# A retention and mixture-of-experts kernel: state products of attention on four quarters of the array, another order of loads and side work

## The chip, the cores and the metric

The kernel runs on one core of a Trainium2 chip. The metric is the device time of one execution in microseconds (us); lower is better. Times of the profile come from one profiled execution.

## What is computed

Three layers follow one another, all in float32: a linear attention with decay (2 batches, 8 heads, 768 positions, head size 64), a layer of 8 experts that every token passes, weighted by a routing matrix, and a dense layer with `h - tanh(h)`. Cut to what matters:

```
attention, block by block:  out  = ((q k^T) * decay) v + (q * lam^i) state
                            state = lam^64 * state + (k * lam^rev)^T v
experts:   P = exp(x w_gate - max);  8 times: P /= rows sum + 1e-9;  P /= column sum + 1e-9;  P *= N/E
           out = sum over e of P[:, e] * (relu(x w1[e]) w2[e])
dense:     h = x w_in;  out = (h - tanh(h)) w_out
```

The kernel takes blocks of 128 positions in place of 64; the formulas hold for any block.

## The kernel before

**Attention.** `N` = 1536 tokens are cut into 12 chunks `c` of 128 positions; even and odd chunks belong to the two batches. A chunk is one row of `qkv`: q, k with heads on the partitions, k with positions on the partitions, v (256 KB each, 1 MB a chunk). `load_chunk` (L186) puts it into one of four buffers, on SP's queue. The program is written out in order, by hand: what an engine is given stays in that order on it. `prep` (L242) multiplies q by the decay for the state product (`qd`, L246) and scales k (`scale_k`, L252) on GpSimd; for chunks 6 to 9 ScalarE scales k. `scores` (L260) makes q k^T on TensorE into two banks, `decay` (L270) multiplies them by the table `dtab` on VectorE (L273). `states` (L281) makes k^T v (L289). `outputs` (L292) adds the state product (L303: the old state by `qd`, for all but the first chunk of a batch) and the scores by v (L308) in one bank, brings the state up to date on VectorE (L320), copies the output to `xr` on ScalarE (L323) and issues the load of chunk c + 4.

In L303 head 2n sits on partitions 0 to 63 of both operands and of the output, head 2n + 1 on 64 to 127, so two of the four quarters of the array are used:

```
for n in range(NP):
    for hh in range(2):
        p = slice(64 * hh, 64 * hh + 64)
        nc.tensor.matmul(out=o[p, n], lhsT=sn[p, n], rhs=qd[c][p, n], ...)
```

A float32 product is two instructions, so a group of 8 products is 16. Ahead of the loop, five products on zeros (`still`, L397) stand between the scores and the output of chunk 0.

**Side work of attention.** After each chunk the tables `blocks` (L378) and `wt` (L383) give out more. The experts use a scheme with seven products in place of eight, on sums and differences of blocks: `raws` (L336) splits blocks of x into a high and a low half (ScalarE the high, VectorE the low one, L150), `sums` (L344) makes the sums on GpSimd, `sblocks` (L353) splits them. `w_load` (L118) loads a weight unit of 1 MB as two DMAs, `w_sum` (L125) makes its sums, `w1_split` (L152) and `w2_split` (L163) split it. `gate1` (L361) and `gate2` (L370) make the routing logits of four chunks.

**Experts.** A loop over 62 slots (L689) makes seven products of 6 instructions (`product`, L673) and 6 output tiles of 6 (`tiles`, L525). Side work is put into four spots of a slot by `put` (L608): `fd`, `fa`, `fb`, `fc` in this order. `stage` (L455) makes the routing matrix in slots 1 to 5, with a column sum by TensorE (L471) and VectorE. `conv` (L494) turns the weights of the dense layer to float32, with steps on VectorE and GpSimd (L514, L515). In slot 0, `pah` is the sum of `pal` and `sa` (L723), `pal` is then added to by the fourth product, and two relus empty the banks (L587).

Of the kernel before, what the change touches and what calls it, by code (L numbers as in the profile page):

```python
# [21 lines left out]
NCH = N // CH  # L22
# [32 lines left out]
def kernel(  # L55
# [17 lines left out]
    psh = ctx.enter_context(tc.tile_pool(name="psh", bufs=4, space=bass.MemoryType.PSUM))  # L73
    psy = ctx.enter_context(tc.tile_pool(name="psy", bufs=1, space=bass.MemoryType.PSUM))
# [42 lines left out]

    def w_load(q):  # L118
# [3 lines left out]
        for i in range(2):  # L122
            nc.sync.dma_start(out=wraw[q][:, 1024 * i:1024 * i + 1024], in_=src[:, 1024 * i:1024 * i + 1024])
# [54 lines left out]
    attq = ctx.enter_context(ExitStack())  # L178
    ap = attq.enter_context(tc.tile_pool(name="att", bufs=1, side="right"))
# [4 lines left out]
    qkvt = {}  # L184

    def load_chunk(c, parts=((0, 2), (2, 4))):  # L186
        if c not in qkvt:
            qkvt[c] = yq.tile([128, 4, 512], F32, tag="qkv", name=f"qkv{c}")
        src = qkv[c].rearrange("p (a n) -> p a n", a=4)
        for i, j in parts:  # L190
            nc.sync.dma_start(out=qkvt[c][:, i:j], in_=src[:, i:j])
# [12 lines left out]
    warm = bank("warm")  # L204
    for i in range(9):
        nc.tensor.matmul(out=warm, lhsT=zero[:, 0:128], rhs=zero, start=True, stop=True)
# [45 lines left out]
    def scale_k(c):  # L252
        kn = qkvt[c][:, 2].rearrange("p (h d) -> p h d", h=H)
# [5 lines left out]

    def scores(c):  # L260
        k = qkvt[c][:, 1].rearrange("p (n i) -> p n i", n=NP)
        sc = [bank(f"sc{c}_{i}") for i in range(2)]
        q = qkvt[c][:, 0].rearrange("p (n i) -> p n i", n=NP)
        for n in range(NP):
            for hh in range(2):
                p = slice(64 * hh, 64 * hh + 64)
                nc.tensor.matmul(out=sc[hh][:, 128 * n:128 * n + 128], lhsT=k[p, n], rhs=q[p, n], start=True, stop=True)
        scps[c] = sc

    def decay(c):  # L270
        a = ap2.tile([128, H, 128], F32, tag="at", name=f"at{c}")
# [619 lines left out]
```

## Time and profile before

| | |
|---|---|
| time, median of 3 runs | 1256.54 us (1256.02 to 1257.32) |
| profiled execution | 1257.17 us, span of the profile 1255.4 us |
| TensorE, weight load, VectorE, ScalarE, GpSimd busy | 99%, 91%, 77%, 44%, 34% of the span |
| attention | from the start to 55.10 us |
| experts | from 55.10 us on, 62 slots |
| DMA | 83.53 MB, mean 67 GB/s; 327 GB/s in the first 31 us |

Busy time is how long an engine has work in it; the ends of products are modelled, and following products overlap, so the time from one start to the next tells more than a duration. In a row of the timeline an idle time in brackets is that ahead of the group, with what ended it; a name that had been done for long stands for something else, often a DMA.

### The profile page before, as it was taken

The page shows a single profiled execution, that of the slowest core. Times are in us where ns is not written, and L with a number is a line of the kernel's source. Part 1 is how long each engine was busy: PE and PEld are TensorE (multiplying, and loading weights), DVE is VectorE, ACT ScalarE, POOL GpSimd, SP SyncE. Part 2 cuts the span into 40 slices and gives each one's busy share as a digit, 9 for nine tenths or more (in the row PEclk, how much of TensorE's full clock was granted, in tenths as well). Part 3 has the DMA queues.
Part 4 walks back from the last instruction along what each step waited for, and adds up shares of the span by engine and source line. Part 5 has one row for each costly group of instructions (what it writes and reads, how often), then busy time and mean ns, then how long its engine had stood idle before and what let it go on. Part 6 is the DMA issues. An engine that isn't in the chain of part 4 may idle for free.

```text
span 1255.4 us, 18456 instructions
## 1 busy us (share of the span) xinstructions
PE 1245.5 (99%) x7031; PEld 1139.2 (91%) x7031; DVE 969.4 (77%) x1874; ACT 547.2 (44%) x1044; POOL 424.6 (34%) x428
## 2 busy tenths in 40 slices
PE   9999999999999999999999999999999999999998
PEld 6889999999999999999999999999999988888887
DVE  6967888778777677777777777767775688898987
ACT  3753333333333333333333333333333578786864
POOL 5832233334433343343334334334332202020200
PEclk9999999999999999999999999999999999999999
DMA  8310112212112221221222112222211111011101
GB/s 327 129 34 34 43 59 74 69 60 72 59 60 85 81 83 59 68 64 59 72 72 72 59 59 73 68 78 90 68 55 34 34 34 34 34 35 34 34 34 67
DMA packets 35658, 83.53 MB, mean 67 GB/s; under 512 B 4209, under 2 KB 12401, under 8 KB 35569
## 3 DMA queue, kind: packets, MB, share of 16 engines
q1 hardware_dynamic: 35424, 82.35, 20.0%
q8 instruction: 55, 0.90, 0.3%
q14 instruction: 35, 0.28, 0.1%
q10 hardware_dynamic: 144, 0.00, 0.0%
HBM read 70.80 MB, written 11.53 MB: 66 GB/s over the span
## 4 chain that ended last, share of the span: by engine, by line
PE 95%; DVE 3%; ACT 2%; DMA 0%; issue 0%; SPq 0%; DVEq 0%; ACTq 0%
PE yq L534 13%; PE yq L536 13%; PE yq L535 13%; PE pal L679 7%; PE pal L681 6%; PE pal L682 6%; PE pbh L681 3%; PE pbh L682 3%; PE pbh L679 3%; PE yp L565 3%; PE g L813 3%; PE yp L563 3%; PE yp L562 3%; PE g L815 3%; PE g L814 3%; PE pbl L681 2%
## 5 line engine op out<-in xcount | busy, mean ns | idle before, releaser
L549 DVE SCALAR_TENSOR_TENSOR yacc<-yq,prob,yacc 128x512 f32<-128x512 f32 x336 | 240.2, 746 | 115.9 <-PE yq L536 115.3
L150 POOL TENSOR_TENSOR w1l<-wsum,w1h 128x1024 fp32r<-128x1024 f32 x31 | 74.1, 2391 | 214.1 <-ACT w1h L148 214.1
L534 PE MATMUL yq<-w2h,h1h 128*128 128x512 f32 x384 | 146.1, 381 | 0.0
L536 PE MATMUL yq<-w2h,h1l 128*128 128x512 f32 x384 | 145.6, 379 | 0.0
L535 PE MATMUL yq<-w2l,h0h 128*128 128x512 f32 x384 | 145.6, 379 | 0.0
L536 PE MATMUL yq<-w2h,h0l 128*128 128x512 f32 x384 | 145.6, 379 | 0.0
L535 PE MATMUL yq<-w2l,h1h 128*128 128x512 f32 x384 | 145.6, 379 | 0.0
L534 PE MATMUL yq<-w2h,h0h 128*128 128x512 f32 x384 | 145.6, 379 | 0.0
L150 POOL TENSOR_TENSOR w2l<-wraw,w2h 128x512 fp32r<-128x512 f32 x80 | 105.9, 1339 | 80.5 <-ACT w2h L148 80.5
L679 PE MATMUL pal<-xsh,w1h 128*128 128x384 f32 x384 | 125.6, 327 | 1.6 <-ACT sa L707 0.9
L682 PE MATMUL pal<-xsh,w1l 128*128 128x384 f32 x384 | 125.2, 326 | 0.0
L681 PE MATMUL pal<-xsl,w1h 128*128 128x384 f32 x384 | 125.2, 326 | 0.0
L587 ACT ACTIVATE h1h<-pah 128x384 fp32r<-128x384 f32 x64 | 31.4, 491 | 184.6 <-PE yq L535 180.0
L514 POOL TENSOR_TENSOR c<-c,d 128x256 f32<-128x256 f32 x64 | 47.4, 741 | 185.0 <-DVE d L513 185.0
L587 ACT ACTIVATE h0h<-pbl 128x384 fp32r<-128x384 f32 x64 | 31.4, 491 | 139.1 <-PE yq L535 139.0
L536 PEld LDWEIGHTS yq<-w2h,h0l 128*128 128x128 f32 x384 | 72.7, 189 | 10.3
L534 PEld LDWEIGHTS yq<-w2h,h0h 128*128 128x128 f32 x384 | 72.7, 189 | 10.3
L535 PEld LDWEIGHTS yq<-w2l,h0h 128*128 128x128 f32 x384 | 72.6, 189 | 10.2
L536 PEld LDWEIGHTS yq<-w2h,h1l 128*128 128x128 f32 x384 | 72.6, 189 | 10.2
L535 PEld LDWEIGHTS yq<-w2l,h1h 128*128 128x128 f32 x384 | 72.7, 189 | 6.9
L534 PEld LDWEIGHTS yq<-w2h,h1h 128*128 128x128 f32 x384 | 72.6, 189 | 6.9
L679 PEld LDWEIGHTS pal<-xsh,w1h 128*128 128x128 f32 x384 | 72.6, 189 | 5.4 <-DVE pah L723 1.0
(220 smaller groups left out, 3253.7 us busy)
## 6 DMA issues: line engine op xcount, KB each, us to landing
wraw<-in_w SPq DMA_DIRECT2D x64, 512.0 KB, 4.9
d<-in_wio SPq DMA_DIRECT2D x64, 256.0 KB, 5.2
qkv<-in_qkv SPq DMA_DIRECT2D x21, 512.0 KB, 7.1
wscr<-c SPq DMA_DIRECT2D x64, 128.0 KB, 1.9
wraw<-wscr SPq DMA_DIRECT2D x16, 512.0 KB, 4.4
out<-yacc SPq DMA_DIRECT2D x12, 256.0 KB, 2.2
qkv<-in_qkv SPq DMA_DIRECT2D x4, 256.0 KB, 5.4
lamb<-in_lam ACTq DMA_DIRECT2D x1, 4.0 KB, 4.9
```

The lines of the kernel that those rows point to most:

```text
L150: eng.tensor_tensor(out=lo, in0=src, in1=hi.bitcast(F32), op=ALU.subtract)
L514: nc.gpsimd.tensor_tensor(out=c1.bitcast(F32), in0=c1.bitcast(F32), in1=lo.bitcast(F32), op=ALU.mult)
L534: nc.tensor.matmul(out=yp, lhsT=hi, rhs=pairs(w2h[q][:, i]), start=i == 1, stop=False)
L535: nc.tensor.matmul(out=yp, lhsT=hi, rhs=pairs(w2l[q][:, i]), start=False, stop=False)
L536: nc.tensor.matmul(out=yp, lhsT=lo, rhs=pairs(w2h[q][:, i]), start=False, stop=i == 0)
L549: nc.vector.scalar_tensor_tensor(out=y, in0=yp, scalar=prob[:, c, q // 4:q // 4 + 1], in1=y, op0=ALU.mult, op1=ALU.add)
L562: nc.tensor.matmul(out=yp, lhsT=a[:, ts], rhs=pairs(w2h[q][:, i]), start=first, stop=False)
L563: nc.tensor.matmul(out=yp, lhsT=a[:, ts], rhs=pairs(w2l[q][:, i]), start=False, stop=False)
L587: nc.scalar.activation(out=hi, in_=ps, func=ACTF.Relu)
L679: nc.tensor.matmul(out=ps, lhsT=w1h[q][:, ws], rhs=pairs(xh[:, k]), start=start and k == 0, stop=False, skip_group_check=True)
L681: nc.tensor.matmul(out=ps, lhsT=w1h[q][:, ws], rhs=pairs(xl[:, k]), start=False, stop=False, skip_group_check=True)
L682: nc.tensor.matmul(out=ps, lhsT=w1l[q][:, ws], rhs=pairs(xh[:, k]), start=False, stop=k == 1, skip_group_check=True)
```

## The change

State products take four quarters of the array: heads are put on the partitions in another order, so that the four products of a set have four pairs of row half and column half. The two row halves write to two banks (`ps[:, 0]`, `ps[:, 1]`), whose upper halves hold the states' new parts and the gate's products. The order in `outputs` becomes scores by v, k^T v, state product, gate. x comes out with its heads in another order, so the rows of `w1` and of the gate's weights are put in that order as they are loaded (`by_head`: four DMAs with pieces of 512 bytes for `w1`, 32 bytes for the gate). q and k of a chunk have a buffer apart from k and v, and q and k are issued a chunk earlier. Weights 0 are issued behind chunk 3, ahead of chunk 4, and their split comes one to three chunks earlier; `w_load(1)` moves from chunk 6 to 4, `w_sum(1)` from 9 to 7. The `still` products go. `decay` is one pass over both banks. `sums(10)` and `raws(7)` move into slot 0 of the experts, the last gate's products from spot `fc` to `fa` of slot 0, `raws(8)` and `sums(11)` from `fc` of slot 0 to `fd` of slot 1. The column sum of the routing matrix is taken by VectorE over the 12 chunks first, and TensorE then sums 8 columns in place of 96. The banks of attention are given back at its end, and the experts' banks wait for them tile by tile.

```diff
+    def by_head(dst, src, n):
+        d, s = (a.rearrange("p (b k f) -> p b k f", b=n, k=2) for a in (dst, src))
+        for e in range(2):
+            for r in range(2):
+                nc.sync.dma_start(out=d[64 * e:64 * e + 64, :, r], in_=s[64 * r:64 * r + 64, :, e])
+
...
-        for i in range(2):
+        if u < NU:
+            by_head(wraw[q][:, 0:1024], src[:, 0:1024], 4)
+        for i in range(u < NU, 2):
             nc.sync.dma_start(out=wraw[q][:, 1024 * i:1024 * i + 1024], in_=src[:, 1024 * i:1024 * i + 1024])
...
-    load_chunk(0, ((0, 1), (1, 2), (2, 4)))
-    for c in range(1, 4):
-        load_chunk(c)
-    nc.sync.dma_start(out=wgt, in_=wg.rearrange("p (k e) -> p k e", e=E))
+    load_chunk(0, (0, 1), (1, 2))
+    load_chunk(1, (0, 2))
+    load_chunk(0, (2, 4))
+    load_chunk(2, (0, 2))
+    load_chunk(1, (2, 4))
+    load_chunk(3, (0, 2))
+    for c in (2, 3):
+        load_chunk(c, (2, 4))
+    by_head(wgt.rearrange("p k e -> p (k e)"), wg, 2)
+    w_load(0)
...
+        q, k = (qkt[c][:, i].rearrange("p (n i) -> p n i", n=NP) for i in range(2))
+        scps[c] = psc.tile([128, 2, 512], F32, tag="sc", name=f"sc{c}")
         for n in range(NP):
-            for hh in range(2):
-                p = slice(64 * hh, 64 * hh + 64)
-                nc.tensor.matmul(out=sc[hh][:, 128 * n:128 * n + 128], lhsT=k[p, n], rhs=q[p, n], start=True, stop=True)
-        scps[c] = sc
+            for r in range(2):
+                p = slice(64 * r, 64 * r + 64)
+                nc.tensor.matmul(out=scps[c][:, r, 128 * n:128 * n + 128], lhsT=k[p, n], rhs=q[p, n], start=True, stop=True)
...
+        at[c] = ap2.tile([128, H, 128], F32, tag="at", name=f"at{c}")
+        nc.vector.tensor_tensor(out=byrow(at[c]), in0=scps.pop(c).rearrange("p r (n i) -> p r n i", n=NP), in1=byrow(dtab),
+                                op=ALU.mult)
...
+        ps = ops[c] = pso.tile([128, 2, 512], F32, tag="o", name=f"o{c}")
+        o = ps[:, :, 0:256].rearrange("p r (a i) -> p r a i", a=2)
+        for i in range(H):
+            a, r, e = i // 4, i // 2 % 2, i % 2
+            h = 4 * a + 2 * e + r
+            nc.tensor.matmul(out=o[64 * e:64 * e + 64, r, a], lhsT=v[:, h], rhs=at[c][:, h], start=a == 0, stop=first,
+                             skip_group_check=True)
+        if carried(c):
+            stp = ps[:, 0, 256:512].rearrange("p (n e) -> p n e", n=NP)
+            for n in range(NP):
+                for r in range(2):
+                    h = 2 * n + r
+                    nc.tensor.matmul(out=stp[64 * r:64 * r + 64, n], lhsT=k[:, h], rhs=v[:, h], start=False, stop=True,
+                                     skip_group_check=True)
...
         if not first:
...
+            for a in range(2):
+                for r in range(2):
+                    for e in range(2):
+                        p, n = slice(64 * r, 64 * r + 64), 2 * a + e
+                        nc.tensor.matmul(out=o[64 * e:64 * e + 64, r, a], lhsT=sn[p, n], rhs=qd[c][p, n], start=False, stop=True,
+                                         skip_group_check=True)
+        gates(c)
...
-                nc.vector.tensor_copy(out=sn, in_=stp.pop(c))
+                nc.vector.tensor_copy(out=sn, in_=stp)
...
+        nc.scalar.activation(out=xr[c].rearrange("p (a r) i -> p r a i", r=2), in_=o, func=ACTF.Copy)
+        for i in (4, 5) if c == 0 else (c + 5,):
+            if i < NCH:
+                load_chunk(i, (0, 2))
         if c + 4 < NCH:
-            load_chunk(c + 4, ((0, 2), (2, 4)) if carried(c + 4) else ((0, 2), (3, 4)))
+            load_chunk(c + 4, (2, 4) if carried(c + 4) else (3, 4))
...
+    def gates(c):
+        b, ps = c // TPB - 1, ops[c][:, 1, 256:512]
+        if b >= 0 and c % TPB == 0:
+            gate1(b, ps)
+        if b >= 0 and c % TPB == 1:
+            gate2(b, ps)
+
+    def gatesc(c):
+        b, ps = c // TPB - 1, ops.pop(c)[:, 1, 256:512]
+        if b >= 0 and c % TPB == 0:
+            gate1c(ps)
+        if b >= 0 and c % TPB == 1:
+            gate2c(b, ps)
...
-        10: [(raws, 6), (sums, 9)], 11: [(raws, 7), (sums, 10)],
+        10: [(raws, 6)], 11: [(sums, 9)],
...
-        1: lambda: w_load(0),
-        3: lambda: (w_sum(0, nc.vector), w1_split(0, 0, which=(0,)), w2_split(0, 0)),
-        4: lambda: w1_split(0, 0, which=(1,)), 5: lambda: w2_split(0, 1), 6: lambda: (w1_split(0, 1), w_load(1)),
-        9: lambda: w_sum(1, nc.gpsimd),
+        2: lambda: (w_sum(0, nc.vector), w1_split(0, 0), w2_split(0, 0)),
+        3: lambda: (w1_split(0, 1), w2_split(0, 1)), 4: lambda: w_load(1), 7: lambda: w_sum(1, nc.gpsimd),
...
     ahead(0)
-    still = psy.tile([128, 512], F32, tag="y3", name="still")
-    for i in range(5):
-        nc.tensor.matmul(out=still, lhsT=zero[:, 0:128], rhs=zero, start=True, stop=True)
+    ahead(1)
     make_lq()
     for c in range(NCH):
         for i in ((1,), (2, 3))[c] if c < 2 else (c + 2,):
             if i < NCH:
...
-        if c == 1:
-            ahead(1)
-            ahead(2)
-        if c > 0:
-            states(c)
         outputs(c)
+        gatesc(c)
...
-        if 0 < c < NCH - 2:
-            scores(c + 2)
-        if c > 0 and c % TPB == 0:
-            gate1(c // TPB - 1)
-        if c > TPB and c % TPB == 1:
-            gate2(c // TPB - 1)
-        if 0 < c < NCH - 2:
-            decay(c + 2)
+        ahead(c + 2)
...
+    psh = ctx.enter_context(tc.tile_pool(name="psh", bufs=4, space=bass.MemoryType.PSUM, reuse_waits="tile"))
+    psy = ctx.enter_context(tc.tile_pool(name="psy", bufs=1, space=bass.MemoryType.PSUM, reuse_waits="tile"))
...
+        box["part"] = sm.tile([128, E], F32, tag="cp", name="cp")
+        nc.vector.tensor_reduce(out=box["part"], in_=prob.rearrange("p t e -> p e t"), axis=AX.X, op=ALU.add)
...
-            nc.tensor.matmul(out=ps[:, 0:NCH * E], lhsT=ones, rhs=prob.rearrange("p t e -> p (t e)"),
-                             start=True, stop=True)
+            nc.tensor.matmul(out=ps[:, 0:E], lhsT=ones, rhs=box.pop("part"), start=True, stop=True)
             cs = sm.tile([128, E], F32, tag="cs", name="cs")
-            nc.vector.tensor_reduce(
-                out=cs, in_=ps[:, 0:NCH * E].rearrange("p (t e) -> p e t", e=E), axis=AX.X, op=ALU.add
-            )
-            nc.vector.tensor_scalar(out=cs, in0=cs, scalar1=1e-9, scalar2=None, op0=ALU.add)
+            nc.vector.tensor_scalar(out=cs, in0=ps[:, 0:E], scalar1=1e-9, scalar2=None, op0=ALU.add)
...
-    put(fc, 0, gate1, NBLK - 1, ybank)
-    put(fc, 0, raws, NCH - 4)
-    put(fc, 0, sums, NCH - 1)
+    gps = {}
+
+    def lastgate(i):
+        if i % 2 == 0:
+            gps[i] = ybank(f"lg{i}")
+        if i == 0:
...
+    put(fa, 0, lastgate, 0)
+    put(fa, 0, raws, NCH - 5)
+    put(fb, 0, lastgate, 1)
+    put(fb, 0, sums, NCH - 2)
     put(fc, 0, sblocks, NCH - 3)
-    put(fd, 1, gate2, NBLK - 1, ybank)
+    for i in (2, 3):
+        put(fd, 1, lastgate, i)
+    put(fd, 1, raws, NCH - 4)
+    put(fd, 1, sums, NCH - 1)
     put(fa, 1, stage, 0)
```

## Rows read from the trace of the kernel before

**Rows 1.** Busy time by stage: us, PE, PEld, DVE, ACT, POOL, granted clock, DMA share, GB/s.

```profile
10.46:55.10 44.64, 43.54 (x756) 37.34 (x756) 39.40 (x79) 26.57 (x71) 35.42 (x33) 1.00 0.72 259
```

**Rows 2.** TensorE in order of time: start us, us, engine, line, operation, count, idle before.

```profile
6.34 2.08 PE L267 MATMUL sc<-qkv 64*128 64x128 f32 x16 [0.87 <-DMA qkv<-in_qkv]
...
8.36 2.10 PE L399 MATMUL still<-zr 128*128 128x512 bf16 x5
...
10.39 1.09 PE L308 MATMUL o<-at,qkv 128*64 128x128 f32 x16
...
19.29 1.16 PE L267 MATMUL sc<-qkv 64*128 64x128 f32 x16
...
20.38 0.69 PE L289 MATMUL stp<-qkv 128*64 128x64 f32 x16
...
20.99 1.09 PE L303 MATMUL o<-qd,st 64*64 64x128 f32 x16
...
22.01 1.09 PE L308 MATMUL o<-at,qkv 128*64 128x128 f32 x16
...
28.41 1.06 PE L365 MATMUL lgT<-xr,wgt 128*8 128x128 f32 x32
...
55.10 0.43 PE L679 MATMUL pal<-xph,w1h 128*128 128x384 f32 x1
```

**Rows 3.** DMA in 40 slices of 0 to 30 us; SP's issues: start us, us.

```profile
GB/s 0 0 115 141 34 165 267 426 421 415 415 421 426 421 415 404 415 371 320 320 289 344 333 246 197 279 393 366 339 377 415 426 388 415 410 382 415 415 284 339
...
12.04 0.80 SPq L191 DMA_DIRECT2D qkv<-in_qkv  x2
```

**Rows 4.** GpSimd in order of time, 19 to 55 us.

```profile
19.31 1.28 POOL L246 TENSOR_TENSOR qd<-qkv,lq 128x512 f32<-128x512 f32 x1 [2.51 <-PE o L308]
...
46.45 1.17 POOL L348 TENSOR_TENSOR xr<-xr,xr 128x256 f32<-128x256 f32 x1
...
50.09 1.50 POOL L246 TENSOR_TENSOR qd<-qkv,lq 128x512 f32<-128x512 f32 x1
...
51.55 0.73 POOL L129 TENSOR_TENSOR wsum<-wraw 128x256 f32<-128x256 f32 x1
...
54.20 1.06 POOL L132 TENSOR_TENSOR wsum<-wraw,wsum 128x256 f32<-128x256 f32 x1
```

**Rows 5.** GpSimd by line and shape, 5 to 80 us: busy us, mean ns, idle before.

```profile
L246 POOL TENSOR_TENSOR qd<-qkv,lq 128x512 f32<-128x512 f32 x10 | 14.7, 1476 | 4.1 <-PE o L308 2.5 <-DVE lq L229 1.0 <-PE o L303 0.6
...
L258 POOL TENSOR_TENSOR qkv<-qkv,dtab 128x512 f32<-128x512 f32 x6 | 6.5, 1079 | 7.1 <-DVE dtab L217 6.5 <-DMA qkv<-in_qkv 0.6
...
L150 POOL TENSOR_TENSOR w2l<-wraw,w2h 128x512 fp32r<-128x512 f32 x3 | 4.2, 1389 | 12.0 <-ACT w2h L148 12.0
```

**Rows 6.** VectorE in order of time, 35 to 53 us.

```profile
35.54 1.28 DVE L273 TENSOR_TENSOR at<-sc,dtab 128x512 f32<-128x512 f32 x2
...
42.37 1.75 DVE L150 TENSOR_TENSOR w1l<-wsum,w1h 128x1024 fp32r<-128x1024 f32 x1
...
51.15 1.28 DVE L273 TENSOR_TENSOR at<-sc,dtab 128x512 f32<-128x512 f32 x2
```

**Rows 7.** Waits of TensorE, 0 to 120 us: us, times, longest.

```profile
PE pal L679 <- ACT sa L707: 0.9, 1, 0.9
...
PE pal L679 <- DVE pah L723: 0.7, 1, 0.7
```

**Rows 8.** ScalarE by line and shape, 5 to 80 us.

```profile
L368 ACT ACTIVATE lt<-lgT 8x128 f32<-8x128 f32 x12 | 3.2, 266 | 2.5 <-PE lgT L365 2.4
```

**Rows 9.** Chain that ended last, in order of time: start us, us.

```profile
95.72 0.31 PE mxB L465 x2
...
104.98 0.19 PE csum L471 x2
```

**Rows 10.** GpSimd in order of time in the experts, 322 to 329 us.

```profile
322.01 0.73 POOL L129 TENSOR_TENSOR wsum<-wraw 128x256 f32<-128x256 f32 x1 [4.43 <-DMA wraw<-in_w]
...
328.10 0.74 POOL L514 TENSOR_TENSOR c<-c,d 128x256 f32<-128x256 f32 x1 [3.18 <-DVE d L513]
```

More of the change, by code (lines that the diff above doesn't have):

```diff
@@ L203 @@
     nc.vector.memset(ones, 1.0)
-    warm = bank("warm")
+    warm = pso.tile([128, 2, 512], F32, tag="o", name="warm")
     for i in range(9):
-        nc.tensor.matmul(out=warm, lhsT=zero[:, 0:128], rhs=zero, start=True, stop=True)
+        nc.tensor.matmul(out=warm[:, 0], lhsT=zero[:, 0:128], rhs=zero, start=True, stop=True)
     nc.vector.memset(bias[:, 3:4], 0.0)
@@ L294, in outputs @@
         first, last = pos == 0, pos == NPB - 1
-        v = qkvt[c][:, 3]
-        sn = st[c % B]
-        o = psy.tile([128, 512], F32, tag=f"y{2 + c % 2}", name=f"o{c}").rearrange("p (n i) -> p n i", n=NP)
-        if not first:
-            for n in range(NP):
-                for hh in range(2):
-                    p = slice(64 * hh, 64 * hh + 64)
-                    nc.tensor.matmul(out=o[p, n], lhsT=sn[p, n], rhs=qd[c][p, n], start=n == 0, stop=False,
-                                     skip_group_check=True)
@@ L305, in outputs @@
-        for n in range(NP):
-            for hh in range(2):
-                h = 2 * n + hh
-                nc.tensor.matmul(
-                    out=o[64 * hh:64 * hh + 64, n], lhsT=v[:, 64 * h:64 * h + 64], rhs=at[c][:, h],
-                    start=first and n == 0, stop=True, skip_group_check=True,
-                )
-        if c == 0:
-            states(0)
+        kv, sn = kvt[c], st[c % B]
+        k, v = (kv[:, i].rearrange("p (h d) -> p h d", h=H) for i in range(2))
+        ps = ops[c] = pso.tile([128, 2, 512], F32, tag="o", name=f"o{c}")
@@ L317, in outputs @@
             else:
[L318 removed]
                 for n in range(NP):
[L320 removed]
+                    nc.vector.scalar_tensor_tensor(out=sn[:, n], in0=sn[:, n], scalar=lq[:, n, 127:128], in1=stp[:, n],
                                                    op0=ALU.mult, op1=ALU.add)
         xr[c] = ap8.tile([128, KT, 128], F32, tag="xr", name=f"xr{c}")
[L323 removed]
+        nc.scalar.activation(out=xr[c].rearrange("p (a r) i -> p r a i", r=2), in_=o, func=ACTF.Copy)
@@ L359, with gate1 @@
     nc.gpsimd.memset(lt, 0.0)
-    def gate1(b, bank=bank):
-        ps = bank(f"lgT{b}")
+    def gate1(b, ps):
         for k in range(KT):
@@ L365, in gate1, with gate1c, gate2, gate2c @@
                 nc.tensor.matmul(out=ps[32 * j:32 * j + E, 0:128], lhsT=wgt[:, k], rhs=xr[TPB * b + j][:, k],
-                                 start=k == 0, stop=k == KT - 1)
+                                 start=k == 0 and b == NBLK - 1, stop=k == KT - 1, skip_group_check=True)
+    def gate1c(ps):
         for j in range(TPB):
             nc.scalar.activation(out=lt[32 * j:32 * j + E], in_=ps[32 * j:32 * j + E, 0:128], func=ACTF.Copy)
-    def gate2(b, bank=bank):
-        ps = bank(f"lg{b}")
-        nc.tensor.matmul(out=ps[:, 0:TPB * E], lhsT=lt, start=True, stop=True,
+    def gate2(b, ps):
+        nc.tensor.matmul(out=ps[:, 0:TPB * E], lhsT=lt, start=b == NBLK - 1, stop=True, skip_group_check=True,
                          rhs=ident.rearrange("p (j r) -> p j r", j=TPB)[:, :, 0:E])
+    def gate2c(b, ps):
         nc.scalar.activation(out=logits[:, TPB * b:TPB * b + TPB], in_=ps[:, 0:TPB * E].rearrange("p (j e) -> p j e", e=E),
                              func=ACTF.Copy)
+    def gates(c):
[10 more added lines that the diff above has]
+            gate2c(b, ps)
     blocks = {
```

55 lines of the change are left out of this document (21 added, 34 removed).

## The prediction

> **What bounds the kernel now.** I read the busy time by stage first. From 10.46 to 55.10 us TensorE is busy for 43.54 of 44.64 us, but VectorE has 39.40 and GpSimd 35.42 [rows 1]. Attention thus has three engines near their limit, and the experts behind it are a stream of TensorE work. I then read TensorE in order of time: twelve chunks follow one another, and the first expert product begins at 55.10 [rows 2]. That instant, call it T, is what the change can move; the 1200 us behind it follow at TensorE's pace. Third, I read GpSimd and VectorE over the same stretch, since time taken from TensorE alone is no time taken from T [rows 4 to 6].
>
> **State products on four quarters (L303).** Today's 16 instructions alternate between two quarters and take from 20.99 to the next group's 22.01, 1.02 us [rows 2]. Ten chunks have them. No row has four quarters. Nearest are the gate's products on four column groups, 32 in 1.06 us, so 0.53 for 16, and L289, 16 with weights as wide in 0.61 us (20.38 to 20.99) [rows 2]. The other end is 1.02, if they do not overlap. I take 0.6, as L289 loads the same width of weights: 10 x 0.42 = 4.2 us less TensorE work, of which only nine chunks lie behind the load discussed below.
>
> **The start.** The five `still` products go (8.36 to 10.39 [rows 2]) and the scores of chunk 1 take their place, so that those of chunks 1 and 2 no longer follow output 0 together. TensorE reaches the scores of chunk 4 at about 18 instead of 19.29: 2.0 us come from `still`, less the waits for VectorE, which now has decay(1) ahead of its scans. The price may be the clock. The scores of chunk 0 take 2.08 us against 1.09 for later ones (19.29 to 20.38), and a `still` product 0.41 us for 512 columns, which is 1.2 GHz; the group at 10.39 is the first at 2.4 GHz [rows 2]. The granted clock reads 1.00 in the stages [rows 1], so here the spacing is what tells. I expect the rise at the same place, since TensorE is as continuously occupied from 6.34 on; a late rise costs at most half of what runs before 18.
>
> **The load order.** Weights 0 (1 MB) now go ahead of chunk 4. Before, chunk 4 was issued at 12.04 [rows 3] and its q was first used at 19.31, after 2.51 us in which GpSimd sat idle [rows 4], which ends with the load and not with the engine named. The 16 slices of 0.75 us up to 12 us add up to 3365 KB, and those up to 19.3 to 5640 KB [rows 3]. Chunk 4's q and k end at 4720 KB, so a load is usable some 920 KB after its bytes. Now they end at 5770 KB: (5770 + 920 - 3365) / 418 KB per us = 8.0 us behind 12, at 20.0 if the queues stay full. The slices between 13.5 and 19.5 sank to 197 because little was queued until 12.04; that gap closes. Half of weights 0 and the gate's weights come in pieces of 512 and 32 bytes, and no row has such loads. From below they cost nothing; from above 1 MB at the slowest slice, 197, which is 2.8 us more. I take 1.0, since a full queue ran at 415 to 426: usable at 21.0. TensorE then idles about 3 us where it had no wait, and is 1.7 us late at the scores of chunk 4.
>
> The Trainium skill ("DMA: Bandwidth & Descriptors", Specifications) puts line rate at pieces of 512 bytes and up. By that rule only the gate's weights would pay, and chunk 4 would be usable near 20.0.
>
> **GpSimd, the next bound.** It has `w_sum(1)` moved ahead of its last two scalings of q (qd), which TensorE needs. The k and v of chunk 4 come 1.05 MB behind its q (2.5 us), at 23.5; scaling k ends at 24.6 (1.08 [rows 5]). What follows on its queue up to qd 11 is 7 x qd, 3 x `sums`, 2 x `w2l`, one scaling of k and one `w_sum`. At the means of [rows 5], with 3.64 for `sums` (46.45 to 50.09) and 3.71 for `w_sum` (51.55 to 55.26) [rows 4], that is 7 x 1.48 + 10.9 + 2.8 + 1.1 + 3.7 = 28.9. At the shortest seen, 1.28 for qd and 4 x 0.73 for the other two [rows 4], it is 9.0 + 8.7 + 2.8 + 1.1 + 2.9 = 24.5. I take 27.3, nearer the upper end, because VectorE works beside it as now. qd 11 is ready at 51.9, 0.3 later than today's 51.59 [rows 4], and only the last state products (0.6) follow: T = 52.5 instead of 55.10.
>
> **The other two at that point.** TensorE: the scores of chunk 4 from 21.0 (1.1), then for chunks 3 to 9 each 1.02 + 0.61 + 0.6 and a later chunk's scores, 1.09 (7 x 3.32 = 23.2), the gate twice (1.06 each, and some 0.6 for its transposed product in all), and 1.6 for each of the last two: 21.0 + 1.1 + 23.2 + 2.7 + 3.2 = 51.2, and about 1 of waits for VectorE. VectorE: decay(7) ended at 36.82 and decay(11) at 52.43, with the low half of weights 0 (1.75) between them [rows 6]. That is now done earlier, as the weights are there earlier. It takes its time there, so decay(7) stays near 36.8; decay(11) ends near 52.43 - 1.7 - 0.3 (one pass over two banks instead of two) = 50.4, and output 11 with its states adds 1.6: 52.0. The three agree within half a microsecond. T is 52.5 by GpSimd: **2.6 us gained**.
>
> **Slots 0 and 1 of the experts.** TensorE waits 0.7 us for `pah` and 0.9 for `sa` [rows 7]. The last gate's products (1.06) move into the first wait, so about 1.0 goes. `sa` was late behind four copies for the gate (266 ns each [rows 8]) and the blocks of chunks 8 and 9, part of which now come half a slot later: 0.9 goes. In return those copies and raws(7) stand ahead of two relus on ScalarE, 1.1 + 0.7 us, so that the bank of `pal` comes free some 1.0 later than slot 1 wants it. Net 0.9 gained, between 1.9 and a loss of 1.
>
> **Routing sums.** The product for 96 columns takes 0.19 us on the chain; one of a single column takes 0.31, both as two instructions [rows 9]. Fewer columns need not be shorter: 0, at best 8 x 0.1 = 0.8. VectorE's passes stay as many; the reduction only moves ahead of the product.
>
> **Weight loads later on.** The 32 loads become five issues each, one half in 512-byte pieces. GpSimd waits 4.43 us for such a load already, and after its sums has 3.18 us until its next work is released [rows 10]. Three more issues of 0.4 [rows 3], and half a weight at the slowest rate (1.4), make 2.6: covered by the 3.18, so nothing. SP's stores and loads queued behind come 1.2 us later; without that cover this would be rival 4.
>
> **The sum.** 2.6 + 0.9 = 3.5. The profiled execution took 1257.17 us (span 1255.4); the median of the runs is 1256.54. That gives 1253.7 on the profile's own scale and **1253.0** against the median.
>
> **The rivals.**
> 1. *Loads at full rate.* If the pieces run like whole rows, chunk 4 is usable at 20.0, GpSimd is less disturbed (24.5 to 26), and T comes down to 50.5 to 51.5, TensorE's bound with chunk 4 one us earlier. With 1.5 from the slots that is 5 to 6 us: 1250.8. For it: full queues ran at 415 and more [rows 3]. Against: VectorE's own 52.0. The sentence of the skill above speaks for it.
> 2. *The idle costs the clock.* TensorE idles from 18 to 21 or later. Only a rise is in the trace, after 4 us of work behind a gap near 1 [rows 2]. If the clock falls there, chunks 3 and 4 run at 1.2 GHz and some 4 us of work take 4 us more, of which about 2 reach T, since GpSimd waits on loads too; with chunk 4 at 22.8 as well, T is 55.5 and the slots give 0.8 at most: 1256.2. The Trainium skill ("TensorE: Matmul & The Clock Gate", Part 1) says an idle array goes back to the lower clock; no row here shows a fall.
> 3. *The quarters don't overlap.* Then 0.42 comes back for each of nine chunks: TensorE ends at 55.0, and 0.9 of the slots with 0.1 of T is left: 1255.5. Against it: four column groups do overlap, at 33 ns an instruction [rows 2].
> 4. *Slower: the weights come late all the way.* GpSimd's conversion steps stand behind its sums. From 3.2 us of delay of a load on they are late; VectorE is in order and empties TensorE's banks, and I put the point from which TensorE stalls at about 5 us. At 5.5 this is 0.5 for each of some 29 loads, 14 us, less the 3.5: 1267. Against it: it needs twice the delay of the upper bound.
>
> **Chances.** GpSimd as the bound 0.40 (1251.5 to 1255), full rate 0.25, clock or late loads 0.20, quarters 0.05, slower 0.10. Two tenths of a per cent, about what a measurement of this kernel can tell from no change, is 2.5 us: faster means below 1254.0. The first case lies there with 0.27, the second wholly, the third with 0.03: faster 0.55. Late loads that add up past 1259 take 0.03 beside the 0.10: slower 0.13. The rest, 0.32, is the same. The range runs from 1249.5 (T 50, slots 1.9) to 1258 (T 56.5 with a fallen clock, nothing in the slots); it leaves out rival 4 and the ends of the others.
>
> **What would show it.** The first `pal` product near 52.5, just behind the last state products, and these just behind a qd 11 that ends near 52. The L303 group in 0.5 to 0.6 us. A wait of about 3 us for q of chunk 4 from 18 to 21. No wait for `sa` in slot 1. GpSimd waiting 5 to 7 us for weights instead of 4.43, with its next step released as now. I am wrong if chunk 4 is there no later than today, if VectorE rather than GpSimd ends last before T, if the spacing of products falls back to 1.2 GHz, or if TensorE shows any new wait behind slot 3.

## The result, and the profile after

The change makes the kernel slower: 1271.0 us in the median (1270.47 to 1272.81), 1.0116 of the time before (95% interval 1.0098 to 1.0133). The profiled execution took 1271.25 us, span 1269.1. The forecast was 1253.0 us, range 1249.5 to 1258.0.

Nearly all of it is lost ahead of the experts: T, the start of the first `pal` product, comes at 67.73 us instead of 55.10, 12.6 later. Taking each slot by the start of its first copy `sa`, slot 0 stands 12.56 us behind the kernel before and slot 1 10.63; the distance then grows to 10.9 at slot 6, 12.9 at slot 12, 13.3 at slot 40 and 13.56 at the end.

The stage from output 0 to T, to be read against [rows 1] (columns as there):

```profile
10.29:67.73 57.44, 43.80 (x741) 37.86 (x741) 37.61 (x71) 26.12 (x71) 34.40 (x34) 0.87 0.59 206
```

TensorE, VectorE and GpSimd have hardly more to do than before, or less (43.54, 39.40 and 35.42 us then), but take 57.44 us instead of 44.64 for it. No engine is near its limit any more: they wait for each other. Whom TensorE and ScalarE wait for, 5 to 68 us (us in total, times, longest):

```profile
PE sc L281 <- DMA qk<-in_qkv: 7.2, 2, 5.6
PE o L372 <- ACT xr L328: 3.0, 2, 1.9
PE o L303 <- ACT kv L270: 2.8, 1, 2.8
PE o L380 <- ACT lt L377: 2.3, 1, 2.3
...
ACT xr L328 <- DVE st L325: 23.8, 8, 11.0
```

Before, the last line did not exist: ScalarE's copy of the outputs waited for TensorE alone. The same view of the kernel before (5 to 62 us), and the copy of chunk 3 in order of time:

```profile
ACT xr L323 <- PE o L308: 20.5, 8, 8.9
...
25.77 1.09 PE L308 MATMUL o<-at,qkv 128*64 128x128 f32 x16
...
26.91 0.60 ACT L323 ACTIVATE xr<-o 128x512 f32<-128x512 f32 x1 [0.27 <-PE o L308]
```

That copy followed its product (25.77 and 1.09) within 0.1 us. In the changed kernel it waits for VectorE's state update in each of eight chunks. Such a sum counts all the idle time ahead of the copies, so 23.8 us is not what the update costs. The changed kernel in order of time, 12 to 36 us, all engines (start us, us, engine, line; idle time before, with what ended it):

```profile
12.41 4.97 SPq L120 DMA_DIRECT2D wraw<-in_w  x4
...
17.42 0.60 SPq L129 DMA_DIRECT2D wraw<-in_w  x1
...
17.60 0.67 PE L317 MATMUL o<-qd,st 64*64 64x128 f32 x16
...
18.14 0.83 SPq L200 DMA_DIRECT2D qk<-in_qkv  x2
...
23.85 2.08 PE L281 MATMUL sc<-qk 64*128 64x128 f32 x16 [5.58 <-DMA qk<-in_qkv]
...
25.86 1.97 PE L303 MATMUL o<-at,kv 128*64 128x128 f32 x16
...
27.81 1.52 DVE L135 TENSOR_TENSOR wsum<-wraw 128x256 f32<-128x256 f32 x1
...
28.61 0.71 PE L317 MATMUL o<-qd,st 64*64 64x128 f32 x16
...
31.11 1.16 DVE L138 TENSOR_TENSOR wsum<-wraw,wsum 128x256 f32<-128x256 f32 x1
...
31.83 0.67 PE L317 MATMUL o<-qd,st 64*64 64x128 f32 x16
...
32.43 0.40 PE L372 MATMUL o<-xr,wgt 128*8 128x128 f32 x6
...
33.13 0.84 DVE L325 SCALAR_TENSOR_TENSOR st<-st,lq,o 128x64 f32<-128x64 f32 x4
...
34.07 0.60 ACT L328 ACTIVATE xr<-o 128x512 f32<-128x512 f32 x1 [11.03 <-DVE st L325]
...
34.72 1.09 PE L372 MATMUL o<-xr,wgt 128*8 128x128 f32 x26 [1.89 <-ACT xr L328]
```

Three things can be read here. SP issues q and k of chunk 4 only at 18.14, behind weights 0, whose four pieces alone take it 4.97 us (12.41), and TensorE waits 5.58 us for them. VectorE's sums of weights 0 (27.81 to 32.2) stand ahead of the state update at 33.13. And the copy of the output of chunk 3 waits for that update, with the gate's products behind it: the last product of this output ends at 29.32 (28.61 and 0.71), the copy starts at 34.07. So 4.75 of the 11.03 us are the update's; the rest is TensorE's late chunk. The experiments tell what each is worth.

### The profile page after: what moved, and what is told of

The parts are those of the page before. It is cut to its first block, busy times and chain, and to the rows that moved or that the text cites. A ratio compares the mean times of both kernels' runs of the same rounds, so it can differ in the third digit from the quotient of the medians.

```text
span 1269.1 us, 18726 instructions
## 1 busy us (share of the span) xinstructions
PE 1245.2 (98%) x7026; PEld 1139.1 (90%) x7026; DVE 969.3 (76%) x1862; ACT 548.9 (43%) x1044; POOL 424.6 (33%) x428
## 4 chain that ended last, share of the span: by engine, by line
PE 89%; DVE 5%; ACT 2%; DMA 2%; SPq 1%; issue 1%; POOL 1%; DVEq 0%; ACTq 0%; POOLq 0%
PE yq L543 12%; PE yq L545 12%; PE yq L544 12%; PE pal L706 6%; PE pal L709 6%; PE pal L708 6%; PE pbh L706 3%; PE pbh L708 3%; PE yp L574 3%; PE pbh L709 3%; PE g L840 3%; PE yp L571 3%; PE yp L572 3%; PE g L842 3%; PE g L841 3%; PE pbl L709 2%
## 5 line engine op out<-in xcount | busy, mean ns | idle before, releaser
L544 PEld LDWEIGHTS yq<-w2l,h0h 128*128 128x128 f32 x384 | 72.6, 189 | 10.3
L543 PEld LDWEIGHTS yq<-w2h,h0h 128*128 128x128 f32 x384 | 72.6, 189 | 10.3
L545 PEld LDWEIGHTS yq<-w2h,h1l 128*128 128x128 f32 x384 | 72.6, 189 | 10.3
L545 PEld LDWEIGHTS yq<-w2h,h0l 128*128 128x128 f32 x384 | 72.6, 189 | 10.3
L135 POOL TENSOR_TENSOR wsum<-wraw 128x256 f32<-128x256 f32 x31 | 22.7, 731 | 170.5 <-DMA wraw<-in_w 170.5
```

The lines of the kernel that those rows point to most:

```text
L543: nc.tensor.matmul(out=yp, lhsT=hi, rhs=pairs(w2h[q][:, i]), start=i == 1, stop=False)
L544: nc.tensor.matmul(out=yp, lhsT=hi, rhs=pairs(w2l[q][:, i]), start=False, stop=False)
L545: nc.tensor.matmul(out=yp, lhsT=lo, rhs=pairs(w2h[q][:, i]), start=False, stop=i == 0)
```

## Experiments

The suspects: the loads (**A**: weights in pieces, more of SP's time), the shared tile (**B**: one tile `ps` holds outputs, new states and gate, read by ScalarE and VectorE), and, once the first runs were in, the early work on weights 0. T and times of all kernels follow. T is that of the profiled execution; each ratio is taken against executions of the kernel before that were timed with it, whose medians lie between 1256.6 and 1257.2:

| kernel | T, us | median us | ratio to before (95% interval) |
|---|---|---|---|
| before | 55.10 | 1256.6 | |
| the change | 67.73 | 1271.0 | 1.0098 to 1.0133 |
| 1 plain loads | 66.74 | 1268.2 | 1.0068 to 1.0102 |
| 2 states in banks of their own | 60.44 | 1263.3 | 1.0034 to 1.0064 |
| 3 = 1 + 2 | 57.35 | 1258.6 | 1.0001 to 1.0019 |
| 4 first pieces on ScalarE's queue | 68.83 | 1272.7 | 1.0105 to 1.0145 |
| 5 copy ahead of the state update | 62.19 | 1265.4 | 1.0055 to 1.0089 |
| 6 weights 0 as before | 61.80 | 1269.8 | 1.0091 to 1.0124 |
| 7 = 1 + 5 | 59.55 | 1260.5 | 1.0016 to 1.0038 |
| 8 = 1 + 5 + 6 | 56.83 | 1258.2 | 1.0001 to 1.0019 |
| 9 = 8 + gate copies ahead | 53.47 | 1253.8 | 0.9963 to 0.9984 |
| 10 before + pieces | 58.48 | 1263.2 | 1.0029 to 1.0061 |
| 11 = 9 with the late copies | 59.80 | 1260.7 | 1.0023 to 1.0047 |
| 12 = 9 with the early weights | 56.04 | 1258.5 | 1.0004 to 1.0024 |

**1. Plain loads.** The host puts the rows of `w1` and of the gate's weights into the new order, and the loads are whole again.

```diff
-        if u < NU:
-            by_head(wraw[q][:, 0:1024], src[:, 0:1024], 4)
-        for i in range(u < NU, 2):
+        for i in range(2):
...
-    by_head(wgt.rearrange("p k e -> p (k e)"), wg, 2)
+    nc.sync.dma_start(out=wgt, in_=wg.rearrange("p (k e) -> p k e", e=E))
```

> The changed kernel with its rows of w1 and of the gate's weights put in the new order by the host's layout, so that each weight load is two DMAs of whole 4 KB rows again and the gate's load one. Theory A (the five issues of a load by heads hold up SP: chunk 4's q and k are issued at 18.1 instead of about 11, TensorE stands 5.6 us and its clock falls, and later the dense layer's loads behind a weight load come late, 2.9 us over the slots): chunk 4's scores begin at 18 to 20 without a fall of the clock behind them, the first pal product comes 6 to 8 us earlier than 67.7, the steps in the slots (2.0 at slot 12, 0.4 at slot 40, 0.25 at slot 6) go, and the time is 1260 to 1263. Theory B (output and states in one bank put ScalarE's copy behind VectorE's state update, and this chain sets the length of attention): the load is only waited for once, the chain is as long as before from there, the first pal product comes at 64 or later, and the time is 1265 to 1267, since only the slots come back.

Measured 1268.2, 2.8 less than the change and above both ranges. TensorE, in order of time:

```profile
21.12 1.90 PE L279 MATMUL sc<-qk 64*128 64x128 f32 x16 [3.14 <-DMA qk<-in_qkv]
```

Chunk 4 comes 2.7 us earlier than with pieces, yet T moves by 1.0 only: TensorE arrives earlier at a chain that is late for another reason. In the slots, slot 12 loses 0.70 instead of 1.97, but in the profiled execution 1.72 us are lost at slot 34, where the change lost nothing (last section). T of 66.74 is what B had forecast (64 or later), so B is the larger cause.

**2. States in banks of their own.** The states' new parts get a tile; to make room, the scores have one pair of banks instead of two.

```diff
-    psc = attq.enter_context(tc.tile_pool(name="psc", bufs=2, space=bass.MemoryType.PSUM))
+    psc = attq.enter_context(tc.tile_pool(name="psc", bufs=1, space=bass.MemoryType.PSUM))
+    pss = attq.enter_context(tc.tile_pool(name="pss", bufs=2, space=bass.MemoryType.PSUM))
...
-            stp = ps[:, 0, 256:512].rearrange("p (n e) -> p n e", n=NP)
+            stp = pss.tile([128, 512], F32, tag="st", name=f"stp{c}")[:, 0:256].rearrange("p (n e) -> p n e", n=NP)
...
-                    nc.tensor.matmul(out=stp[64 * r:64 * r + 64, n], lhsT=k[:, h], rhs=v[:, h], start=False, stop=True,
+                    nc.tensor.matmul(out=stp[64 * r:64 * r + 64, n], lhsT=k[:, h], rhs=v[:, h], start=n == 0, stop=True,
```

> The changed kernel with the states' new parts in a bank of their own (two such banks; the scores then have one pair of banks instead of two). Loads by heads stay. Theory B: ScalarE's copy of an output no longer waits for VectorE's state update, its scaling of k and its copies for the gate come earlier, and TensorE's waits for the copy, for scaled k and for the gate's copies (3.0, 2.8 and 2.3 us) go: 6 to 9 us less before the first pal product, 1262 to 1265. Theory A: those waits came only from the late load and from the half clock; they shift elsewhere, at most 2 us less, 1269 or more. The single pair for the scores may cost up to 1 us.

Measured 1263.3, 7.7 less, as B had it. TensorE's waits, 5 to 62 us:

```profile
PE sc L282 <- DVE at L289: 5.7, 3, 2.4
PE sc L282 <- DMA qk<-in_qkv: 4.9, 2, 3.2
```

No wait of TensorE for ScalarE is left. The first line comes from the single pair of score banks, so 7.7 may understate the tile; by how much, this run does not show.

**3. Both.**

> Both of these: layout by the host, and states in a bank of their own. If A and B together are all that went wrong, what was forecast for the quarters should be seen: first pal product at 50 to 53, no fall of the clock, 1250 to 1254. If TensorE's clock or GpSimd's queue is a third cause, the first pal product stays at 55 or later and the time is 1255 to 1259.

Measured 1258.6, in the range that stood for a third cause. The wait for chunk 4 is gone, since TensorE itself comes to it later (its scores start at 21.25 without idle time, 21.12 in run 1). TensorE waits 7.2 us for VectorE to empty the only pair of score banks, the longest time 3.74 behind the sums of weights 0.

**4. The first pieces on ScalarE's queue.** The gate's weights and weights 0 are issued there, so that SP is free for chunk 4.

> The changed kernel with the first loads by heads (the gate's weights and the first half of weights 0) issued on ScalarE's queue instead of SP's; the pieces and their bytes are the same. If the time of SP's issues is what made chunk 4 late, its q and k are issued by 9 us and land by 16 to 19, and the first pal product comes 4 to 7 us earlier: 1264 to 1267, as the later loads stay on SP. If the small pieces themselves slow the DMA engines, chunk 4 lands at 22 to 24 as now, and the time stays at 1270 to 1272.

Measured 1272.7: no faster than the change. Chunk 4 was waited for 0.39 us only, but now k and v of chunk 0 (1.97 us, to 10.96) and q and k of chunk 2 (2.38 us, to 15.62) came late, and from 10 to 15 us the DMA engines moved 205 GB/s at full share (1.13) instead of 379 at 1.01 in the kernel before. SP's time is thus not all of it: the pieces take the DMA engines' time, whoever issues them.

**5. The copy ahead of the state update.** In `outputs` the lines of ScalarE's copy move ahead of VectorE's update. Nothing else.

```diff
         gates(c)
+        xr[c] = ap8.tile([128, KT, 128], F32, tag="xr", name=f"xr{c}")
+        nc.scalar.activation(out=xr[c].rearrange("p (a r) i -> p r a i", r=2), in_=o, func=ACTF.Copy)
         if not last:
...
-        xr[c] = ap8.tile([128, KT, 128], F32, tag="xr", name=f"xr{c}")
-        nc.scalar.activation(out=xr[c].rearrange("p (a r) i -> p r a i", r=2), in_=o, func=ACTF.Copy)
```

> The changed kernel with one edit: in every chunk ScalarE's copy of the outputs is issued ahead of VectorE's state update, so that in the bank that both read it is VectorE that waits for ScalarE (copy 0.60 us) and no longer ScalarE for VectorE; loads, banks and weights stay. Theory bank (the copy's wait for the state update, which stands behind VectorE's other work, is most of the lost time): the waits of the copy on VectorE go, the first pal product comes near 61 instead of 67.7, and the time is 1261 to 1265. Rival (any order of the two on one bank costs the same, the wait only passes to VectorE, which is as full): 1268 to 1272.

Measured 1265.4, T 62.19, 0.4 us above the theory's range and clear of the rival's. The order of two lines is worth 5.6 us. The gate's copies, still behind the update, wait for it now: those to `lt` 5.9 us in two places, those to `logits` 1.8 in two.

**6. Weights 0 as before.** `w_load(0)` behind chunk 1, and the table `wt` of the kernel before.

> The changed kernel with weights 0 as in the kernel before: loaded after chunk 1, sums and splits of weights 0 spread over chunks 3 to 6, weights 1 loaded at chunk 6 and summed at chunk 9; banks and by-head loads stay. Theory load order and VectorE's early weights work together: chunk 4's queries and keys are issued some 5 us earlier, the wait of 5.58 us for them falls under 1 us, and no sums stand ahead of decay 5, so the first pal product comes at 59 to 62 and the time is 1262 to 1266. Rival (the shared bank alone sets the end, whatever VectorE does ahead of the state update): 1268 to 1271.

Not as expected: T falls to 61.80 as the theory had it, and chunk 4 is waited for 0.29 us; but the median is only 1.2 us lower, and its runs spread from 1266.9 to 1272.0. The profiled one is the fastest (1266.92, span 1264.8), and even there 4.6 us are lost again behind slot 1, in steps at slot 12 (1.97), slot 18 (1.62) and later.

**7. Plain loads, copy ahead.**

> The changed kernel with the order of e5_order and the plain loads of e1_plain (the host lays the rows out, no by-head pieces); both pairs of score banks stay, weights 0 stay early. If the 7.2 us in which TensorE waited for the single pair of score banks in e3_both were a cost of that experiment alone: first pal product at 54 to 56, time 1254 to 1257. If VectorE's early work on weights 0 (sums of 1.2 to 1.5 us each instead of 0.42 before) is what is left: 57 to 58 as in e3_both, 1257.5 to 1260.

Measured 1260.5, T 59.55, above both ranges: with both pairs of score banks the kernel is not faster than run 3. The gate's copies still stand behind the update here, so the tile costs more than the order of this one copy. What the 7.2 us of waits cost run 3 this run can't tell; run 12, which is this kernel with the gate's copies ahead, comes to 1258.5 and T 56.04, against 1258.6 and 57.35.

**8. All three.**

> The changed kernel with all three taken back or mended: copy ahead of the state update, plain loads, weights 0 loaded and worked on as in the kernel before. What is left of the change is the quarters, the moved scores and slots, and the routing sums. If the three are all that was lost, the prediction's sum of 3.5 us holds for the rest: first pal product at 52 to 54, time 1252.5 to 1255.5. If the rest has a cost of its own (the clock at half after a gap, single tiles), 1256 to 1260.

Measured 1258.2. T is 56.83, not 52 to 54, so something was left. All engines of this kernel, 31 to 37 us:

```profile
31.24 0.60 ACT L318 ACTIVATE xr<-o 128x512 f32<-128x512 f32 x1
...
33.95 0.84 DVE L324 SCALAR_TENSOR_TENSOR st<-st,lq,o 128x64 f32<-128x64 f32 x4
...
34.83 0.20 ACT L381 ACTIVATE logits<-o 128x32 f32<-128x32 f32 x1 [2.99 <-DVE st L324]
34.92 2.00 ACT L267 ACTIVATE kv<-kv,dtab 128x64 f32<-128x64 f32 x8
36.03 1.09 PE L300 MATMUL o<-at,kv 128*64 128x128 f32 x16 [2.46 <-ACT kv L267]
```

The gate's copy of 0.20 us waits 2.99 us for the state update, ScalarE's scaling of k stands behind it, and TensorE waits for k. The gate's columns lie in the second bank of `ps`, the new states in the first: what the two share is the tile. Run 9 moves the gate's copies alone.

**9. The gate's copies ahead, too.** The edit against run 8:

```diff
         nc.scalar.activation(out=xr[c].rearrange("p (a r) i -> p r a i", r=2), in_=o, func=ACTF.Copy)
+        gatesc(c)
         if not last:
...
         outputs(c)
-        gatesc(c)
```

> The version with copy ahead of the state update, plain loads and weights 0 as before, and one more edit: ScalarE's copies of the gate's results (chunks 4, 5, 8, 9) are issued ahead of VectorE's state update too, since in the run without it they waited 3.0, 2.5 and 0.9 us for that update, and the key scaling of the next chunk stood behind them (TensorE waited 2.46 and 1.97 us for scaled keys). Theory (every copy out of the tile that the state update reads waits for it, and those waits are the rest of the loss): no such wait is left, the first pal product comes at 53 to 54.5 instead of 56.8, slots 0 and 1 stand 2 to 3 us earlier than before, and the time is 1253.5 to 1255.5, below the kernel before. Rival (GpSimd's queue, full from 39 to 57 us, sets the end whatever ScalarE does): first pal product 56 to 57, time 1257 to 1258.5.

Measured 1253.8, 0.26% faster than before (0.16% to 0.37%), and T 53.47. All engines, 48 to 55 us:

```profile
49.52 1.47 POOL L257 TENSOR_TENSOR qd<-qk,lq 128x512 f32<-128x512 f32 x1
...
50.53 1.21 DVE L285 TENSOR_TENSOR at<-sc,dtab 128x1024 f32<-128x1024 f32 x1
...
51.84 1.09 PE L300 MATMUL o<-at,kv 128*64 128x128 f32 x16 [0.59 <-issue]
...
52.87 0.67 PE L314 MATMUL o<-qd,st 64*64 64x128 f32 x16
...
53.47 0.43 PE L705 MATMUL pal<-xph,w1h 128*128 128x384 f32 x1
```

qd 11 is ready at 50.99, decay 11 at 51.74, and output 11 follows 0.1 us later: VectorE is the bound here. Slot 1 stands 3.60 us ahead of the kernel before, more than the 2 to 3 expected; 0.9 of it is lost at slot 12.

**10. The kernel before with pieces.** The loads of `w1` alone are cut as in the change; the gate's weights stay whole.

> The kernel before with one part of the change alone: the first half of each weight load is issued in four pieces of 64 rows with runs of 512 bytes, as the change does, instead of one plain transfer (the host lays the rows out so that the same weights arrive); the gate's weights stay plain. Theory (the pieces cost time of SP's queue and of the DMA engines all the way): the start moves by under 1.5 us, since weights 0 come in behind chunk 1, and then steps of 0.4 to 2 us come in where a slot's loads stand behind the weights in SP's queue (slot 12 and two or three later ones), 1258 to 1261. Rival (3.18 us of slack of the weight loads covers them as the prediction said): 1256 to 1257.5.

Measured 1263.2, 6.5 us slower, more than the theory's 1258 to 1261 (runs from 1259.5 to 1265.7). T is 3.4 us late, 2.94 of it one wait for a chunk behind weights 0 (to 29.99). Then slot 12 loses 2.46, and later slots 0.3. All engines, 205 to 223 us:

```profile
205.51 3.39 SPq L122 DMA_DIRECT2D wraw<-in_w  x4
...
208.94 0.60 SPq L131 DMA_DIRECT2D wraw<-in_w  x1
...
210.06 0.98 SPq L505 DMA_DIRECT2D d<-in_wio  x2
...
215.58 0.32 DVE L514 TENSOR_SCALAR c<-d 128x256 int32<-128x256 int32 x1 [2.61 <-DMA d<-in_wio]
```

and TensorE behind it:

```profile
222.28 0.43 PE L687 MATMUL pbh<-xsh,w1h 128*128 128x384 f32 x1 [2.19 <-DVE h1l L596]
```

SP is held 4.0 us by one weight unit (0.80 before, 202.13 to 202.93), the load `d` behind it comes late, VectorE waits for it in `conv`, and `h1l` stands behind that. Rates of the same five microseconds, before and with pieces (us; busy us of PE, PEld, DVE, ACT, POOL; granted clock; DMA share; GB/s):

```profile
20.00:25.00 5.00, 5.00 (x93) 4.28 (x91) 3.42 (x9) 1.94 (x4) 3.90 (x4) 1.00 1.01 389
```

```profile
20.00:25.00 5.00, 4.63 (x86) 3.87 (x86) 3.26 (x8) 1.48 (x3) 2.13 (x3) 1.00 1.09 256
```

**11 and 12. One part back into version 9.** First the order of the copies, then the early weights:

> The version of e9_gates with one part of the change put back: ScalarE's copies (outputs, gate) are issued behind VectorE's state update again, out of the tile that both read; plain loads and weights 0 as before stay. Theory (the wait for the shared tile has a price of its own, since VectorE's state update stands behind its weights and hi-lo work in nearly every chunk): first pal product 59 to 63 instead of 53.5, time 1260 to 1264. Rival (that wait costs only where the early weights hold VectorE up, so that with the weights as before it is worth under 3 us): first pal product 54 to 56.5, time 1254.5 to 1257.

> The version of e9_gates with another part of the change put back: weights 0 loaded at the start and worked on in chunks 2 and 3, weights 1 loaded at chunk 4 and summed on GpSimd at chunk 7; plain loads and copies ahead of the state update stay. Theory (early weights cost on two queues: SP issues chunk 4's queries and keys some 2.5 us later, TensorE waits about 3 us for them; VectorE's four sums take 5.4 us beside GpSimd's key scaling instead of 1.7 and stand ahead of decay 5): first pal product 55.5 to 57.5 instead of 53.5, 1256 to 1258. Rival (both are hidden by what VectorE and GpSimd do less of later on): 53 to 54.5, 1253.5 to 1255.

The late copies cost 6.9 us (1260.7, T 59.80): as the theory had it, without any early weights. ScalarE's waits of that run, 5 to 62 us:

```profile
ACT xr L325 <- DVE st L322: 16.3, 8, 4.0
```

The early weights cost 4.7 us (1258.5, above the expected range; T 56.04, within it). TensorE, in order of time:

```profile
21.23 2.08 PE L279 MATMUL sc<-qk 64*128 64x128 f32 x16 [3.13 <-DMA qk<-in_qkv]
...
55.44 0.67 PE L315 MATMUL o<-qd,st 64*64 64x128 f32 x16 [0.96 <-POOL qd L258]
56.04 0.43 PE L704 MATMUL pal<-xph,w1h 128*128 128x384 f32 x1
```

The last state product waits for qd 11 on GpSimd, the bound that the prediction had put at T. In the profiled execution 1.7 us of the loss come at one stroke at 542 us (last section).

Tile 6.9, early weights 4.7 and pieces 6.5 (measured on the kernel before) make 18.1, and from version 9 to the change there are 17.2. All three taken out, nothing of the loss is left, but that does not mean that their costs add. With the late copies in place (run 11, 1260.7), early weights bring it to 1268.2 (run 1), pieces to 1269.8 (run 6, with its wide spread) and both to 1271.0: 7.5, 9.1 and 10.3. So early weights and pieces largely hide behind each other, and taken out of the change alone, pieces gave back only 2.8 us and early weights 1.2.

## Why the prediction was wrong

**What bounds the kernel, and the state products: right.** T was the instant that moved most. L317 takes 0.60 us from start to start (31.83 to 32.43), the value taken.

**The missing step: a wait that the change adds.** The prediction costed the new place of the states and the gate at nothing, and did not ask who reads the tile. ScalarE's copy and VectorE's update had had tiles of their own; now one follows the other in the order in which they are written, and VectorE's update stands behind sums, splits and the decay of a later chunk. This alone costs 6.9 us (run 11). The list of what would make the prediction wrong looked for new waits behind slot 3; this one is ahead of slot 0. The Trainium skill ("PSUM — Partial Sum Buffer", PSUM bank collisions raise a hardware error) says that two engines must not be on one bank and quadrant at once, two reads included, and that the compiler's scheduler puts such accesses in order: a rule that bore on this change and was not weighed. The trace agrees for the outputs, one half of which shares a bank with the new states (4.75 us of wait, to 34.07); the gate's copies wait as well, though their bank is another.

**The load order: mechanism right, size wrong.** A wait of about 3 us for chunk 4, to 21.0, was forecast: 20.0 for full queues, 1.0 for the pieces. It ends at 23.85 after 5.58 us, past the upper bound of 22.8. With whole rows it ends at 21.12 and 21.23 (runs 1 and 12), so the first term was 1.1 short and the second 1.7: the pieces cost 2.7. The forecast held only "if the queues stay full", and they did not. The eight pieces of the gate's weights and weights 0 took SP 4.62 us (from 7.04) and 4.97 us (from 12.41), some 1.2 us an issue; later pieces took 0.65, where 0.4 was assumed. Behind them the DMA engines ran short of work. The change, and run 1 with whole rows (columns as in [rows 1]):

```profile
15.00:20.00 5.00, 3.27 (x68) 2.81 (x64) 3.40 (x8) 1.89 (x4) 3.97 (x4) 1.00 0.68 162
```

```profile
15.00:20.00 5.00, 2.98 (x64) 2.55 (x62) 3.63 (x8) 2.18 (x4) 4.02 (x4) 1.00 1.02 398
```

And where the engines did have a full share, pieces moved less: 256 GB/s where 389 were before (run 10). Rival 1 falls with it. So does the sentence of the Trainium skill ("DMA: Bandwidth & Descriptors", Specifications) beside it, line rate at pieces of 512 bytes and up: pieces of 512 bytes did not run at line rate here (these 256 GB/s).

**The clock: rival 2's mechanism.** After the idle 5.58 us the scores of chunk 4 and the output of chunk 3 take 2.08 and 1.97 us instead of 1.16 and 1.09; the granted clock from 23.8 to 29.2 reads 0.54, the lower of its two levels for nearly all of it. That is some 2 us of TensorE in a stretch whose end VectorE and ScalarE set. The clock falls again just ahead of T, after a wait of 2.26 us for ScalarE's copies for the gate. TensorE in order of time, and that stretch with its granted clock of 0.50 (columns as in [rows 1]):

```profile
62.99 1.97 PE L303 MATMUL o<-at,kv 128*64 128x128 f32 x16
64.90 1.13 PE L317 MATMUL o<-qd,st 64*64 64x128 f32 x16
```

```profile
62.90:66.20 3.30, 3.30 (x38) 2.55 (x36) 2.72 (x5) 1.85 (x5) 0.00 (x0) 0.50 0.02 5
```

From there to T the last two outputs take 4.74 us, and 3.24 in run 11 (56.56 to 59.80): 1.5 us that go into T, near the 2 of rival 2. But here it is a wait for ScalarE that costs the clock, not the load. The clock was not separated from the waits: after the load it is low in runs 1 and 12 too (1.90 and 2.08 us for the scores of chunk 4).

**GpSimd and VectorE at T.** Qd 11 was forecast for 51.9 and came at 60.66 (59.39 and 1.27), since GpSimd waited for TensorE in its turn: 1.52 us for L317 just ahead of it, to get the buffer back. Where the tile's wait is gone and the early weights stay (run 12), GpSimd is the bound as forecast, with qd 11 ready at 55.38, 3.5 us later than forecast. For VectorE the prediction moved the low half (1.75 us) out of the way, but not the four sums into it: beside GpSimd's work they took 4.4 us (27.81 to 32.2) and stood ahead of the state update of chunk 3 and of decay 5.

**Slots, routing sums, later weights.** Slots 0 and 1 gained 1.93 us, the upper end of the forecast (0.9, between 1.9 and -1): the gate's products fill the wait for `pah`, and the wait for `sa` is gone. The routing sums gave nothing (0.01 us in slots 3 to 5), as said. The weights behind slot 3 were costed at nothing, covered by GpSimd's 3.18 us [rows 10]; that cover was read on the wrong queue. Who had no slack was the load `d` on SP behind them, and 2.0 us came in at slot 12 (2.46 in run 10). Not all of that is the pieces': with whole rows 0.70 stays there (run 1). Rival 4 had the sign and the transfers, but neither this chain nor its size: it put 0.5 us on each of 29 loads.

**The sum.** With tile, pieces and early weights mended (run 9) the rest of the change gives 1253.8 and T 53.47, where the prediction had 1253.0 and 52.5 for all of it. That the two are so near is in part luck. T gained 1.6 us and not 2.6, slots 0 and 1 gained 2.0 and not 0.9, and 0.9 was lost at slot 12, which was not forecast. The bound was VectorE (decay 11 at 51.74, forecast 50.4) and not GpSimd, which in run 9 makes the sums of weights 1 only behind qd 11. What was costed at nothing, or sized wrongly, came to 17 us.

**Open.** Whether bank or tile makes the wait for the outputs was not separated. No run takes out the four quarters alone, so that their gain is known from the group's time (0.60 us instead of 1.02) and not from the kernel's. The spread of the runs with pieces (5 to 6 us in runs 6 and 10) and the 0.5 to 0.9 us that slot 12 loses with whole rows (runs 3, 8 and 9) were not followed up.

## What to carry to other kernels

When a change moves two results into one tile of the accumulation banks, list every engine that reads it, in program order: a short copy written behind a busy engine's update inherits that engine's whole queue, and here moving up the lines of all such copies gave the time back. Costs of pieces, issues and moved side work are to be laid on the queue that has no slack (here SP's loads behind the weights, and VectorE's decay), not on the engine that looks fullest. Costs can hide behind each other: taken out alone, pieces gave back 2.8 us and early weights 1.2, and both together 10.3. And a change that loses may hold a gain: taking its parts back one after the other found 0.26% in this one.

## What the runs showed of the hardware

In two runs one step of VectorE took as long as the step of GpSimd beside it. All engines of run 12, 541 to 546 us:

```profile
542.34 2.38 POOL L154 TENSOR_TENSOR w1l<-wsum,w1h 128x1024 fp32r<-128x1024 f32 x1 [4.58 <-ACT w1h L152]
542.40 2.60 DVE L525 SCALAR_TENSOR_TENSOR c<-d,c 128x256 f32<-128x256 f32 x1 [0.46 <-DVE d L524]
...
545.71 0.48 PE L541 MATMUL yq<-w2h,h1h 128*128 128x512 f32 x1 [1.44 <-DVE yacc L556]
```

The step starts 0.06 us behind GpSimd's and takes 2.60 us; in run 9 the same step started 0.30 ahead of GpSimd's and took 0.47. TensorE paid 1.44 us, and the slots behind stand 1.70 later to the end. In run 1 the same step started 0.08 behind (553.13 and 553.05) and took 2.59: the 1.72 us at slot 34. In the same way a sum of 256 columns took 0.42 us with GpSimd idle (run 9, 25.35 us) and 1.2 to 1.5 beside it (27.81 and 31.11 above), while the one at 29.25 of the changed kernel, in a gap of GpSimd (29.04 to 29.49), took 0.41. A shift of one engine against the other by a few tenths of a microsecond was thus worth more here than many a step that the change moved.
